# Lightning attention feeding a two-layer network: from the seventh chunk couple on, attention in two TensorE groups per couple, two state buffers, a new order of loads, some early casts on VectorE

## The chip, the cores and the metric

One core of one Trainium2 chip. The metric is the device time of one execution in microseconds (us), as the median of several. Executions of one kernel on one chip mostly agree within a few tenths of a per cent (at the widest the kernel before took 216.96 to 218.66 us on one chip). Chips differ by a few tenths too: the kernel before had medians of 217.1 to 217.9 us in the four sets of runs below. So small differences are read from the ratios to the kernel before on the same chip.

## The reference

Attention with a decaying state over 4 batches, 8 heads, 768 positions of 64 values; its output is 3072 tokens of 512 values, which go through a two-layer network:

```python
intra = einsum(q_block, k_block) * decay_mask        # "s", then the mask
intra = einsum(intra, v_block)                       # "c"
inter = einsum(q_block * lam**(i+1), kv_state)       # "n"
out_block = intra + inter
kv_state = lam**block * kv_state + einsum(k_dec, v)  # "u", then a sum
...
x = out.transpose(...).reshape(3072, 512)
h = x @ w_in                                         # 512 x 2048: first layer, L1
g = where(h >= 1, h, where(h <= -1, 0, (h+1)**2/4))  # relu on ScalarE, rest on VectorE
return g @ w_out                                     # 2048 x 512: second layer, L2
```

## The kernel before

The kernel takes 24 chunks of 128 positions as 12 couples m = 0 to 11, two per stage of the network from couple 0 on (stage 0 is couples 0 and 1, and so on). The program is written by a list scheduler in Python: every piece of work is an operation with an engine, a modelled duration, what it needs and a due time, and the modelled time at which it starts sets its place in its engine's queue. On the chip only the queues and the semaphores count.

Small matmuls of attention run in a 64x64 tiling, in groups. Before, each couple from 1 on had three: A (n of one half and the scores of one chunk), B (the other scores and n), C (scores times v, from couple 3 on with the state product u of the next couple; the first four products are groups of their own). A block, below, is what the first layer puts into one buffer (four matmuls of 512 columns or eight of 256), or four 512-wide matmuls of the second layer.

```python
def f_u(m):                                   # state product of couple m
    ...
        pl, nm = (..., ((pp_s, "ps"), (pp_t, "pt")))[min(m, 2)][i]
        pu[i] = pl.tile([128, HP, D], F32, name=nm, tag=nm)
    ...                                       # 32 (or 16) matmuls of 64x64

def f_sum(c):                                 # VectorE: PSUM -> state
    if c % NCB == 0:
        nc.vector.tensor_copy(state, pu[c % 2])
    else:
        nc.vector.tensor_tensor(state, state, pu[c % 2], op=AX.add)

def f_ub(c):                                  # ScalarE: bf16 copy of the state, read by n
    ...
    nc.scalar.copy(out=ub[c % NUB], in_=state)
...
# what an L1 block needs: its xT, its weights, and the relu two blocks back (two "ph" buffers)
[("x", ...), ("w", 0, ...), ("m", 1, 0) if n1 < 2 else ("r", n1 - 2), ("l1", n1 - 1)]
...
# due times run backwards from the users of a result
d = [u.due - u.ns - x.extra - LAT for u in users[x.key] if not u.dma]
x.due = min(d + ([x.own] if x.own is not None else []), default=1e9)
```

PSUM, the memory into which every matmul of this kernel writes and from which ScalarE and VectorE read, is full with eight buffers: two "ph" (first layer), two "py" (second layer), "ps" and "pt" (scores or state product, one each), two "px" (attention's output, which ScalarE casts to xT, the first layer's input). In the profile, sc are the masked scores, gT is the second layer's input and osb the output copy.

## Time and profile before

217.12 us median of six (217.03 to 217.34). Marks of TensorE's timeline:

| mark | before, us |
|---|---|
| first L2 block starts | 37.27 |
| group A of couple 5 starts | 82.83 |
| end of the span | 215.8 |
| waits of TensorE for another engine after 38 us | 0.3 |

Profile lines have the source line of the kernel that they belong to (L441), the engine, the operation, what it writes and reads, and in brackets what ended the idle time ahead of it. TensorE (PE) is busy to the end, and after 38 us it waits for almost nothing.

### The profile page before, as it was taken

What the parts mean: (1) busy time and instruction counts of PE and PEld (TensorE: products, weight loads), DVE (VectorE), ACT (ScalarE), POOL (GpSimd) and SP (SyncE); (2) the same over time, 40 slices, a digit from 0 to 9 for tenths busy, and PEclk for the clock granted to TensorE, in tenths of its full rate; (3) what the DMA queues carried; (4) which work ended last, traced back from release to release, by engine and by line L of the source; (5) the groups of instructions that cost most, each with busy time, mean ns of one, the idle gap of its engine ahead of it and who ended that gap; (6) DMA issues with size and microseconds to landing.
All of it is one profiled execution on the core that took longest, in us unless ns stands there. A gap on an engine that the chain in (4) does not pass through costs nothing.

```text
span 215.8 us, 5410 instructions
## 1 busy us (share of the span) xinstructions
PE 202.4 (94%) x2285; PEld 117.6 (54%) x2314; DVE 150.3 (70%) x235; ACT 116.5 (54%) x201; POOL 55.6 (26%) x60
## 2 busy tenths in 40 slices
PE   6887897999999999999999999999999999999993
PEld 4455685666646777667544444544544444444442
DVE  4684887998961999689999688775666655464301
ACT  3556686348536677662956547664644544555020
POOL 4070260069252844267154008000000000000000
PEclk9999999999999999999999999999999999999999
DMA  5999999999998999899998956621101101110022
GB/s 158 290 218 201 271 191 196 226 294 242 166 284 176 243 246 217 203 227 283 242 202 226 263 135 209 101 73 52 49 0 52 49 3 49 49 49 21 31 97 97
DMA packets 64586, 34.43 MB, mean 160 GB/s; under 512 B 20402, under 2 KB 61618, under 8 KB 64562
## 3 DMA queue, kind: packets, MB, share of 16 engines
q1 hardware_dynamic: 60336, 29.89, 62.1%
q0 software_dynamic: 4224, 4.19, 12.4%
q8 instruction: 18, 0.29, 0.6%
q14 instruction: 6, 0.05, 0.1%
q10 hardware_dynamic: 2, 0.00, 0.0%
HBM read 27.26 MB, written 6.29 MB: 155 GB/s over the span
## 4 chain that ended last, share of the span: by engine, by line
PE 88%; DVE 6%; issue 2%; ACT 2%; POOL 0%; POOLq 0%; DVEq 0%
PE ph L441 37%; PE py L489 35%; PE ph L151 3%; PE px L390 3%; PE ps L362 2%; PE px L374 2%; DVE sc L423 2%; PE py L483 1%; PE ps L403 1%; DVE w L466 1%; DVE ks L294 1%; ACT xT L430 1%; ACT qT L334 1%; PE pt L324 1%; DVE gT L471 1%
## 5 line engine op out<-in xcount | busy, mean ns | idle before, releaser
L441 PE MATMUL ph<-xT,w_in_sb 128*128 128x256 bf16 (+1 forms) x570 | 94.5, 308 | 1.3 <-ACT xT L430 1.1
L450 ACT ACTIVATE r<-ph,one 128x512 bf16<-128x512 f32 x96 | 65.7, 688 | 52.5 <-PE ph L441 46.8
L489 PE MATMUL py<-w_out_sb,gT 128*128 128x512 bf16 x345 | 86.5, 379 | 2.4 <-issue 1.7
L441 PEld LDWEIGHTS <-w_in_sb 128*128 128x128 bf16 x576 | 54.9, 98 | 31.2 <-issue 1.2
L489 PEld LDWEIGHTS <-gT 128*128 128x128 bf16 x368 | 34.5, 98 | 37.8
L460 DVE TENSOR_SCALAR t<-r 128x1024 bf16<-128x1024 bf16 x48 | 25.8, 538 | 22.0 <-ACT r L450 22.0
L471 DVE TENSOR_TENSOR gT<-w,t 128x1024 bf16<-128x1024 bf16 x48 | 39.9, 832 | 1.3
L466 DVE TENSOR_TENSOR w<-r,t 128x1024 bf16<-128x1024 bf16 x48 | 39.0, 813 | 1.4
L302 POOL TENSOR_TENSOR qs<-x0f,tab_q 128x512 bf16<-128x512 f32 x21 | 24.4, 1181 | 41.5 <-DMA x0f<-in_q_dram 32.4
L294 POOL TENSOR_TENSOR ks<-x1f,tab_p 128x512 bf16<-128x512 f32 x18 | 22.8, 1284 | 25.7 <-PE pt L403 21.1
L423 DVE TENSOR_TENSOR sc<-ps,causal 128x512 bf16<-128x512 f32 x23 | 15.9, 689 | 14.1 <-PE pt L362 12.4
L494 ACT COPY osb<-py 128x512 f32<-128x512 f32 x23 | 13.5, 585 | 17.3 <-PE py L489 15.3
L430 ACT CAST xT<-px 128x512 bf16<-128x512 f32 x24 | 13.1, 586 | 9.5 <-PE px L390 8.6
L423 DVE TENSOR_TENSOR sc<-pt,causal 128x512 bf16<-128x512 f32 x22 | 15.0, 680 | 0.0
L317 ACT CAST v<-x2f 128x512 bf16<-128x512 f32 x24 | 13.7, 619 | 0.2
L151 PE MATMUL ph<-ident 128*128 128x512 bf16 (+1 forms) x39 | 9.5, 381 | 1.6 <-POOL ident masks.py:199 1.6
L362 PE MATMUL ps<-qT,kT 64*64 64x128 bf16 x184 | 10.8, 220 | 0.0
L418 ACT CAST ub<-state 128x256 bf16<-128x256 f32 x19 | 7.7, 406 | 5.0 <-DVE state L411 3.5
L362 PEld LDWEIGHTS <-kT 64*64 64x64 bf16 x384 | 7.8, 106 | 4.0 <-issue 3.8
L362 PE MATMUL pt<-qT,kT 64*64 64x128 bf16 x176 | 9.8, 219 | 0.0
L374 PE MATMUL px<-qT,ub 64*64 64x128 bf16 x152 | 6.4, 222 | 2.0 <-ACT xT L430 1.9
L390 PEld LDWEIGHTS <-v 64*64 64x64 bf16 x384 | 5.8, 106 | 4.5 <-issue 4.4
(59 smaller groups left out, 84.6 us busy)
## 6 DMA issues: line engine op xcount, KB each, us to landing
x0f<-in_q_dram SPq DMA_DIRECT2D x12, 512.0 KB, 6.7
x1f<-in_k_dram SPq DMA_DIRECT2D x12, 512.0 KB, 6.2
x2f<-in_v_dram SPq DMA_DIRECT2D x12, 512.0 KB, 7.0
out_dram<-osb SPq DMA_DIRECT2D x23, 256.0 KB, 2.3
w_in_sb<-in_moe_w_in_dram POOLq DMA_DIRECT2D x4, 512.0 KB, 6.6
w_out_sb<-in_moe_w_out_dram POOLq DMA_DIRECT2D x4, 512.0 KB, 11.0
kT<-ks SPq DMA_TRANSPOSE x18, 4.0
out_dram<-osb SPq DMA_DIRECT2D x1, 192.0 KB, 1.9
```

The source lines that it names most:

```text
L151: nc.tensor.matmul(hot[0][:, :w], lhsT=ident, rhs=_bc(ident, 1, w // 128), start=True, stop=True)
L294: eng.tensor_tensor(ho(ks[c])[:, bs], hs(qkv_ld[c, 1])[:, bs], ho(_bc(tab, 2, D))[:, bs], op=AX.mult)
L302: eng.tensor_tensor(ho(qs[m, e])[:, bs], hs(qkv_ld[m, 0][:, :, e])[:, bs], ho(_bc(tab_q[:, e, m % (NCB // 2), :], 2, D))[:, bs], op=AX.mult)
L362: nc.tensor.matmul(pst[a, r][HD[i], b, :], lhsT=kT[a][HD[r], b, HD[i]], rhs=q_cols(2 * m + i, b, HD[r]), start=True, stop=True)
L423: nc.vector.tensor_tensor(sc_sb[c][:, g], pst[c, g], _bc(causal2[:, c % 2], 1, HP), op=AX.mult)
L430: nc.scalar.copy(out=o, in_=px[:, c % 2].rearrange("p h (e j) -> p h j e", e=2))
L441: nc.tensor.matmul(ph[:, j * m:(j + 1) * m], lhsT=w_in_sb[:, ko, (ni + j) * 128:(ni + j + 1) * 128], rhs=xT[s][:, ko, tok], start=(ko == 0 ...
L450: nc.scalar.activation(out=o, in_=x, func=AF.Relu, bias=one[:, 0:1])
L460: nc.vector.tensor_scalar(t, r, 0.5, 1.0, op0=AX.mult, op1=AX.min)
L466: nc.vector.tensor_tensor(w, r, t, op=AX.subtract)
L471: nc.vector.tensor_tensor(gT[s][:, f - RW * n:f, tok].rearrange("p (a b) m -> p a b m", a=RW), w.rearrange("p a (b m) -> p a b m", m=m), t ...
L489: nc.tensor.matmul(py_t[s, ms], lhsT=gT[s][:, ko, ms * 128:(ms + 1) * 128], rhs=w_out_sb[:, ko, :], start=(ko == 0), stop=(ko == FO - 1))
```

## The change

Its intent, as the diff reads: six tiling-mode groups fewer, since each costs time beside its matmuls; a state sum that need not wait for the copy of the last one; and a start with less on ScalarE (two copies of kT, not shown, move to VectorE as well). Cut to its core:

```diff
+    PAIRED = 6
-    ORDER = [0, 1, (0, 0), ...]                 # order of the loads
+    ORDER = [('lq', 0), ('lk', 0), ...]
+    V_DVE, X_DVE, UB_DVE = (2,3,4,5), (0,1), (2,3)
-    state = const.tile([128, HP, D], F32)
+    state = [const.tile([128, HP, D], F32, name=f"state{i}") for i in range(2)]
-    LDD, STD = 25000, 3000                      # due times of loads, groups, transposes ...
+    LDD, STD = 16000, 3000
...
 def f_u(m):
+            ... ((pp_h, "ph"), (pp_y, "py")))[3 if m >= PAIRED else min(m, 2)][i]
+def f_b(m, more):
+    if m < PAIRED:
+        f_s(2 * m + 1, 1)
+    else:
+        f_n(m, 1); f_s(2 * m + 1)
+    if more: f_u(m + 1)                          # u moves from group C into group B
...
 def f_ub(c):
+    src = pu[0] if c % NCB == 0 else state[c % 2]   # first chunk of a batch: straight from PSUM
...
-    PARTS = {1: 2, 2: 2, 4: 1}
+    PARTS = {1: 2, 2: 2, 3: 2, 4: 1}             # L1 of stage 3 in 256-wide halves
```

From couple 6 on the groups are B (n, scores, u of the next couple) and C (scores times v, n, scores of the next couple). Scores of the next couple now live in "ps" and "pt" while u is made, so u goes to "ph" and "py".

## The prediction

> **What bounds the kernel now.** I read the page first (shares, slices, chain), then the TensorE's waits from 38 us on, then its timeline row by row.
>
> ```profile
> span 215.8 us, 5410 instructions
> ...
> PE 202.4 (94%) x2285; PEld 117.6 (54%) x2314; DVE 150.3 (70%) x235; ACT 116.5 (54%) x201; POOL 55.6 (26%) x60
> ...
> PE   6887897999999999999999999999999999999993
> ...
> PE 88%; DVE 6%; issue 2%; ACT 2%; POOL 0%; POOLq 0%; DVEq 0%
> ```
>
> TensorE is the bound. Only the first eight slices (43 us) have holes; after them it works to the end. What it waited for, first over the whole run, then from 38 us on (us in total, times, longest):
>
> ```profile
> PE px L374 <- ACT xT L430: 1.9, 2, 1.5
> ...
> PE ph L441 <- ACT xT L430: 1.1, 1, 1.1
> PE pt L324 <- ACT qT L334: 0.7, 1, 0.7
> PE pt L331 <- ACT qT L334: 0.7, 1, 0.7
> ```
> ```profile
> PE py L489 <- issue: 1.7, 11, 0.2
> PE px L374 <- ACT xT L430: 0.3, 1, 0.3
> ```
>
> So after 38 us a wait of TensorE for another engine costs 0.3 us in all. What an attention group costs is read from the starts of the rows around it:
>
> ```profile
> 161.37 1.03 PE L441 MATMUL ph<-xT,w_in_sb 128*128 128x512 bf16 x4
> 162.32 0.31 PE L374 MATMUL px<-qT,ub 64*64 64x128 bf16 x8
> ...
> 166.34 0.24 PE L362 MATMUL ps<-qT,kT 64*64 64x128 bf16 x1
> ...
> 166.81 1.04 PE L489 MATMUL py<-w_out_sb,gT 128*128 128x512 bf16 x4
> ...
> 169.50 0.64 PE L390 MATMUL px<-sc,v 64*64 64x128 bf16 x32
> 170.07 1.04 PE L441 MATMUL ph<-xT,w_in_sb 128*128 128x512 bf16 x4
> ```
>
> Four 512-wide matmuls take 0.86 us where one feed-forward block follows another, but 0.95 (161.37 to 162.32) where a 64x64 group follows. The group of 32 value products takes 0.57 us (169.50 to 170.07); eight steps of four parallel tiles at 0.053 us (128 columns, a quarter of 0.216) would be 0.43. The group of 16 score and 8 state products takes 0.47 (166.34 to 166.81) for six steps, 0.32. So each group costs 0.09 on entering and 0.14 inside, some 0.235 us, for being a group.
>
> Last, how fast ScalarE frees a PSUM buffer:
>
> ```profile
> 139.31 1.07 ACT L430 CAST xT<-px 128x512 bf16<-128x512 f32 x2
> 140.27 1.15 ACT L317 CAST v<-x2f 128x512 bf16<-128x512 f32 x2
> ...
> 142.88 0.40 ACT L418 CAST ub<-state 128x256 bf16<-128x256 f32 x1
> ...
> 144.90 0.69 ACT L450 ACTIVATE r<-ph,one 128x512 bf16<-128x512 f32 x1 [0.73 <-PE ph L441]
> ```
>
> The first-layer block behind the last row began at 143.77: its relu starts 1.1 us after the block's start and ends 0.69 later. TensorE follows 0.05 after a release (xT ended at 26.07, the matmul started at 26.12). A buffer is therefore reusable 1.83 us after its block began; a block lasts 0.86. With two "ph" buffers that is hidden; with one it is not.
>
> **What the Trainium skill says.** "TensorEngine Tiling (Array Packing)", Key Properties: changing the tiling mode drains TensorE. The trace agrees, with the 0.235 us above. "PSUM — Partial Sum Buffer", Terms and Engine vs sequencer instructions: eight banks, a matmul's output stays within one, ScalarE's and VectorE's queues are strict FIFO and matmuls complete in program order. The kernel uses all eight (ph 2, py 2, pt, ps, px 2), so a new tile in "ph" takes a buffer from the first layer. The trace before shows the FIFO order (the casts above stand ahead of relus), but never a lack of "ph".
>
> **The change, part by part.**
>
> 1. Groups. Couples 6 to 11 had three each (n+s, s+n, c with the next u; s scores, n query times state, c scores times v, u the state product). Now two: s+n with the next u; c with the next s and n. Matmuls are the same. Six groups fewer: 6 x 0.235 = -1.4 us, all on the path.
>
> 2. Early order. The first L1 block now comes before the score group of couple 1; its xT casts move to VectorE, where they queue behind two k casts, two v casts and a q cast. Adding VectorE's rows (masks 0.61 each, casts 0.65, copies 0.4) I get the second xT at 18.7 us and L1 at 18.8 instead of 19.18; but the group of 0.46 us that was done then now follows, so nothing is won. The 1.1 us wait for xT stays (the next L1 really needs it now). The two qT waits (0.67 each) go, since L1 blocks now stand between the transposes. About -1.4 us by the first second-layer block.
>
> 3. First layer of stage 3 in 256-wide halves: 16 matmuls take 1.75 us where 8 wide ones take 1.73; eight times, +0.15. The small waits at 100-104 us (0.45 with issue) should go: -0.45.
>
> 4. The cost. For couples 6 to 11 the state product is put in "ph" and "py" instead of "ps" and "pt", as these now hold scores. In the built program I looked up which bank each tile has and what each wait names. While the product of couple 6 is held, three L1 blocks in a row get the same bank. Hand arithmetic with the durations above:
> - Couple 6: the first L1 after the group waits for a relu that stands behind the ub copy, which waits for the group: 0.1+0.31+0.69+0.05 = 1.15. Two L1 in one bank with four L2 matmuls between: 1.83-1.72 = 0.11. Two directly: 1.83-0.86 = 0.97. Then an L2 block takes the "py" buffer that an output copy must first empty, and this copy stands behind two xT and two v casts that follow group c: release 3.45 after c starts, against 1.65 of own work: 1.8.
> - Couple 7: 0.3 (a relu behind a ub copy), 0.97, 0.11, then L1 waits for a relu behind an output copy and two xT casts: 2.6-0.84 = 1.76.
> - Couple 8: 0.11 + 0.45. Couple 9: about 0.2 (masks on VectorE ahead of the state copy). Couple 10: an L1 waits for a relu behind an output copy: 3.2-1.72 = 1.48. Couple 11: 0.11.
> Sum: 4.0 + 3.1 + 0.6 + 0.2 + 1.5 + 0.1 = 9.5 us. TensorE has no slack there, so all of it is on the path.
>
> 5. Two state buffers let the second sum start without waiting for the first's ub copy: shorter holding, no path. The v and state casts on VectorE early on only shift load; the DMA has its loads and transposes landed 1 to 2 us before the new, earlier use (for couple 6: 87.1 in the trace before, used at about 89).
>
> Sum: 217.05 - 1.4 - 1.4 + 0.15 - 0.45 + 9.5 = 223.4; I say 223.2.
>
> **Rivals.** (a) The plan works: no buffer waits, only parts 1 to 3: 217.05 - 3.1 = 214.0. For it: the change is plainly meant so, and its many constants look tuned. Against: the waits are in the program, engines are in order, and the scheduler's need list for L1 and L2 blocks doesn't name the state product as a holder of their buffer. (b) The start is the main effect, for instance VectorE, busy 15.1 of the 19 us from 19 to 38, becomes the bound there by the moved casts: some 1.5 us of casts could cost 1 to 2 and take the qT gain away: 225. Against: its idle time there (1.3 us before 27.8) covers most. (c) Only the direct single-buffer waits bite, while ScalarE, 54% busy, has its casts done sooner than I think: stalls of 5 us, total 219. For it: a stall early shifts what follows and may hide the next. Against: the long ones hang on casts that cannot start before group c ends.
>
> **Range and chances.** The sum of the gains is sure to about 1 us, that of the stalls to about 2.5. That gives 219.6 to 226.5. Slower by over 2% begins at 221.4, a little under the middle: 0.70. Within 2% needs rival (c) or (a): 0.27. Faster by over 2% (under 212.7) would need more than all gains and no stall: 0.03.
>
> **What would show it.** In the changed kernel's waits from 80 us on: TensorE's L1 line waiting for ScalarE's relu by 6 to 7 us in about a dozen waits, and its L2 line for the output copy, one of about 1.8 us. The 64x64 groups from couple 6 on: two per couple, 0.7 and 0.9 us long. TensorE's slices 16 to 30 no longer all 9. Before 80 us: no wait of transposes for qT, the first L2 block at about 35.9 (37.27 before). It is wrong if the L1 waits are under 3 us, or if the start moves by more than 2 us either way.

## The result, and the profile after

223.34 us median of six (223.13 to 224.61) against 217.12: a ratio of 1.0295, 95% interval 1.0271 to 1.0319. (A ratio is the mean time of one kernel's runs over that of the other's in the same rounds, so not quite the ratio of the medians quoted. Executions over 1.5% slower than the fastest of the same kernel are left out of the means.) All runs were at a granted clock of 0.997 or above.

The page of the changed kernel, its shares and TensorE's 40 slices of 5.5 us:

```profile
PE 203.7 (92%) x2356; PEld 124.4 (56%) x2382; DVE 152.0 (69%) x245; ACT 110.8 (50%) x191; POOL 53.5 (24%) x60
...
PE   7889799999999997778799999799999999999994
```

Slices 16 to 20 (83 to 110 us) and 26 (138 to 144) have holes that were not there. What TensorE waited for from 38 us on (total, times, longest):

```profile
PE ph L457 <- ACT r L466: 5.9, 6, 1.5
PE py L505 <- ACT osb L510: 1.5, 1, 1.5
PE py L505 <- issue: 0.6, 4, 0.2
```

L457 is the first layer, L466 its relu, L505 the second layer, L510 the output copy: 7.4 us of waits for ScalarE that free a PSUM buffer, where there had been none. The first of these waits, in TensorE's timeline after group B of couple 5 (which ends with u of couple 6):

```profile
85.61 1.03 PE L457 MATMUL ph<-xT,w_in_sb 128*128 128x256 bf16 x8 [1.14 <-ACT r L466]
86.70 0.81 PE L505 MATMUL py<-w_out_sb,gT 128*128 128x512 bf16 x3
87.42 1.03 PE L457 MATMUL ph<-xT,w_in_sb 128*128 128x256 bf16 x8
89.28 1.03 PE L457 MATMUL ph<-xT,w_in_sb 128*128 128x256 bf16 x8 [0.82 <-ACT r L466]
...
95.31 1.02 PE L505 MATMUL py<-w_out_sb,gT 128*128 128x512 bf16 x4 [1.50 <-ACT osb L510]
```

The first-layer blocks at 87.42 and 89.28 have no other block between them: their starts are 1.86 apart, where 0.86 would be the block alone. They share one buffer, since the other is held. By whom, VectorE's timeline shows:

```profile
92.88 0.69 DVE L439 TENSOR_TENSOR sc<-ps,causal 128x512 bf16<-128x512 f32 x1 [0.67 <-PE pt L364]
93.49 0.41 DVE L424 COPY state<-ph 128x256 f32<-128x256 f32 x1
93.82 0.68 DVE L439 TENSOR_TENSOR sc<-pt,causal 128x512 bf16<-128x512 f32 x1
94.42 0.41 DVE L426 TENSOR_TENSOR state<-state,py 128x256 f32<-128x256 f32 x1
```

The state copy that empties "ph" stands between two masks (L439). They mask the scores of couple 6, which are made in group C of couple 5; that group began at 91.97. The product had been done at about 84.5. VectorE's own queue thus holds a first-layer buffer for 9 us, though the copy takes 0.41. It was put there by the scheduler: the sum is needed only by the next n, two groups later, so its due time is late, and nothing tells the scheduler that a buffer of the first layer hangs on it.

By the marks:

| mark | before | after | difference |
|---|---|---|---|
| first L2 block | 37.27 | 35.69 | -1.58 |
| A of couple 5 | 82.83 | 81.35 | -1.48 |
| from there to the end | 132.97 | 140.05 | +7.08 |

The marks add up to 5.6 us, the medians differ by 6.2: the profiled execution of the kernel before took 217.55 us, 0.4 above its median, that of the changed kernel 223.13. So the marks of the start may be some tenths too good for the changed kernel.

### The profile page after: what moved, and what is told of

Its sections match the earlier page's. It is cut to its first block, busy times and chain, and to the rows that moved or that the text cites. A ratio compares the mean times of both kernels' runs of the same rounds, so it can differ in the third digit from the quotient of the medians.

```text
span 221.4 us, 5549 instructions
## 1 busy us (share of the span) xinstructions
PE 203.7 (92%) x2356; PEld 124.4 (56%) x2382; DVE 152.0 (69%) x245; ACT 110.8 (50%) x191; POOL 53.5 (24%) x60
## 4 chain that ended last, share of the span: by engine, by line
PE 50%; issue 2%; ACT 2%; DVE 0%
PE py L505 24%; PE ph L457 21%; PE px L395 1%; ACT r L466 1%; PE py L499 1%; PE ps L364 1%; PE px L377 1%; PE ph L499 0%; PE ph L409 0%; ACT xT L446 0%; PE pt L364 0%; PE py L409 0%; DVE osb L517 0%; ACT osb L510 0%
## 5 line engine op out<-in xcount | busy, mean ns | idle before, releaser
L457 PE MATMUL ph<-xT,w_in_sb 128*128 128x256 bf16 (+1 forms) x635 | 95.4, 293 | 7.4 <-ACT r L466 5.9
L466 ACT ACTIVATE r<-ph,one 128x512 bf16<-128x512 f32 x96 | 65.8, 688 | 59.0 <-PE ph L457 42.8
L505 PE MATMUL py<-w_out_sb,gT 128*128 128x512 bf16 x347 | 86.7, 379 | 3.1 <-ACT osb L510 1.5
L457 PEld LDWEIGHTS <-w_in_sb 128*128 128x128 bf16 x640 | 61.1, 98 | 34.0 <-issue 8.7
L505 PEld LDWEIGHTS <-gT 128*128 128x128 bf16 x368 | 35.3, 98 | 38.4 <-issue 1.8
L482 DVE TENSOR_TENSOR w<-r,t 128x1024 bf16<-128x1024 bf16 x48 | 40.9, 853 | 1.5
L487 DVE TENSOR_TENSOR gT<-w,t 128x1024 bf16<-128x1024 bf16 x48 | 38.5, 801 | 1.5
L476 DVE TENSOR_SCALAR t<-r 128x1024 bf16<-128x1024 bf16 x48 | 24.3, 507 | 20.7 <-ACT r L466 20.5
L439 DVE TENSOR_TENSOR sc<-ps,causal 128x512 bf16<-128x512 f32 x23 | 15.9, 690 | 24.9 <-PE pt L364 19.1
L296 POOL TENSOR_TENSOR ks<-x1f,tab_p 128x512 bf16<-128x512 f32 x18 | 21.0, 1189 | 15.9 <-PE ph L409 8.3
L510 ACT COPY osb<-py 128x512 f32<-128x512 f32 x23 | 13.5, 586 | 18.3 <-PE py L505 17.3
L446 ACT CAST xT<-px 128x512 bf16<-128x512 f32 x22 | 11.9, 588 | 8.4 <-PE px L395 7.0
L439 DVE TENSOR_TENSOR sc<-pt,causal 128x512 bf16<-128x512 f32 x22 | 15.0, 682 | 0.0
L319 ACT CAST v<-x2f 128x512 bf16<-128x512 f32 x20 | 11.6, 621 | 1.4 <-PE px L395 0.9
L364 PE MATMUL ps<-qT,kT 64*64 64x128 bf16 x184 | 9.7, 218 | 0.0
L395 PE MATMUL px<-sc,v 64*64 64x128 bf16 x384 | 8.6, 219 | 0.6 <-DVE sc L439 0.6
L434 ACT CAST ub<-state 128x256 bf16<-128x256 f32 x14 | 5.6, 402 | 5.1 <-DVE state L426 5.1
```

The lines of the kernel that those rows point to most:

```text
L296: eng.tensor_tensor(ho(ks[c])[:, bs], hs(qkv_ld[c, 1])[:, bs], ho(_bc(tab, 2, D))[:, bs], op=AX.mult)
L364: nc.tensor.matmul(pst[a, r][HD[i], b, :], lhsT=kT[a][HD[r], b, HD[i]], rhs=q_cols(2 * m + i, b, HD[r]), start=True, stop=True)
L395: nc.tensor.matmul(px[HD[g], i, j, :], lhsT=v_sb[(2 * m + e) % NV][HD[i], 2 * j + g, :], rhs=sc_sb[2 * m + e][HD[i], r, b, :], start=(c % ...
L439: nc.vector.tensor_tensor(sc_sb[c][:, g], pst[c, g], _bc(causal2[:, c % 2], 1, HP), op=AX.mult)
L457: nc.tensor.matmul(ph[:, j * m:(j + 1) * m], lhsT=w_in_sb[:, ko, (ni + j) * 128:(ni + j + 1) * 128], rhs=xT[s][:, ko, tok], start=(ko == 0 ...
L466: nc.scalar.activation(out=o, in_=x, func=AF.Relu, bias=one[:, 0:1])
```

## The experiments

The theory was that the held buffers cost about 8.9 us after couple 5 (8.3 in single stalls that the trace shows, the rest in many of 0.1), that six groups fewer give 1.4 back and the start gives 1.5. Rivals: the longer groups themselves, or a changeover into pairing, cost the time; VectorE has no room; the start is the cost. All twelve runs gave correct results. Edits are against the changed kernel.

### Pairing off, pairing alone, pairing later, stage 3 as before

```diff
# e1_three_groups
-    PAIRED = 6
+    PAIRED = 12
# e2_pair_only: all constants of the start and PARTS as before the change, and
-    V_DVE, X_DVE, UB_DVE = (2,3,4,5), (0,1), (2,3)
+    V_DVE, X_DVE, UB_DVE = (), (), ()
# e3_pair_from_8
-    PAIRED = 6
+    PAIRED = 8
# e4_stage3_wide
-    PARTS = {1: 2, 2: 2, 3: 2, 4: 1}
+    PARTS = {1: 2, 2: 2, 4: 1}
```

> The changed kernel with three groups for every couple; its new order of loads, early casts, two state buffers and 256-wide stage 3 stay. Theory (the state product held in the first and second layers' PSUM buffers costs some 8.9 us, six groups fewer give back 1.4, the start gives 1.5): 223.3 - 8.9 + 1.4 = 215.8, within 1.2, with the waits of the first and second layer for ScalarE after 38 us under 1 us together. Rival (the start, with casts on VectorE, or the two state buffers slow it): stays above 221.

Measured: 216.54 us (ratio to before 0.9958, interval 0.9942 to 0.9975). Waits of L1 and L2 for ScalarE after 38 us: 0.3. The start, with the halves of stage 3, is no cost but a gain, of 0.9 by the ratio; pairing is the cost, 6.8 us by the medians and 7.3 by the ratios. The run is 0.7 above the expectation: the gain of the start is smaller than the 1.5 of the theory, and the stalls are too (the table below).

> The changed kernel with all constants of the start put back (order of loads, due times, v, x and state casts on ScalarE, stage 3 in whole blocks): pairing and two state buffers are left. Theory: 217.1 + 8.9 - 1.4 = 224.6, within 2, since other due times move which blocks meet a held buffer; first-layer waits for relu of 5 us or more after 80 us. Rival (the start is the cost): 217 or less.

Measured: 223.05 us (1.027; 1.024 to 1.030). The start undone, the loss stays, 1.5 below the middle of the expectation and within its range. The second sign, waits of 5 us or more for relu, did not come. The waits have other names here: of the first layer's 5.8 us after 38 us, 3.2 are for the state copies themselves, 1.6 for relu, 1.0 for xT.

> The changed kernel with pairing from couple 8 on in place of 6. Theory: the stalls of couples 6 and 7 (3.9 and 2.9 us by the trace) go and two groups (0.47) come back: 223.3 - 6.8 + 0.5 = 217.0, within 1.5. Rival 1 (each pairing costs the same, by its longer groups: 7.1 us over six couples, 1.2 each): 223.3 - 2.4 = 220.9. Rival 2 (the first paired couple pays for the changeover, wherever it lies): about 220.

Measured: 215.93 us (0.9928; 0.9912 to 0.9944), 1.1 below the middle of the expectation, within its range, and below three groups. Neither rival fits: four couples are still paired, and a changeover is still there. In the trace only 0.3 us of first-layer waits for ScalarE are left after 38 us. So even the stall of 1.4 us that the changed kernel had at couple 10 is gone, although couple 10 is still paired.

Yet the copies come late here too. Two rows of TensorE's timeline and one of VectorE's:

```profile
115.09 1.05 PE L457 MATMUL ph<-xT,w_in_sb 128*128 128x256 bf16 x8
116.92 1.03 PE L457 MATMUL ph<-xT,w_in_sb 128*128 128x256 bf16 x8
121.00 0.41 DVE L426 TENSOR_TENSOR state<-state,ph 128x256 f32<-128x256 f32 x1
```

The product of couple 8 was done at about 115.2, so its buffer was held for 6 us, and no block waited for it: a second-layer block stands between the two first-layer blocks, and their starts, 1.83 apart, are about as far as one buffer needs. A held buffer thus cost time here only where the order of blocks asked for the other one sooner.

> The changed kernel with the first layer of stage 3 in whole 512-wide blocks again. Theory (halving costs 0.15 us of matmul time and the stalls hang on the buffers, not on the width): 223.2, within 0.8. Rival (the halved blocks with their later inputs meet the held buffers and make the stalls of couples 6 and 7): 219 or less.

Measured: 223.04 us (1.0251; 1.0183 to 1.0319), but in two pairs, 221.4 to 221.8 and 224.3 to 224.4 (the trace is one of the slower pair). All four are above the 219 of the rival, so the width is not the cause; what sets the pairs apart was not found. Which wait shows the cost does change, as TensorE's waits from 38 us on tell (two more, not shown, are 1.0 for xT and 0.6 for issue):

```profile
PE ph L457 <- DVE state L426: 4.4, 3, 2.8
PE ph L457 <- DVE state L424: 3.2, 2, 2.2
```

With other blocks in between, a first-layer block is given the state product's own buffer and waits for the state copy itself (7.6 us in all), instead of for the relu in the one other buffer. The holder is the same, only the name differs.

### The state copies first

If holding is what costs, it must be enough to move the copies in VectorE's queue, with groups, matmuls and buffers as they are. One line in the scheduler, after all due times are set, does it (cut to the lines that matter; e6 also changes the need of ub accordingly):

```diff
# e5_copies_first: state sums from couple 6 on get due = -1
-        left = {x.key: len(x.needs) for x in ops}
+        left = {x.key: (len(x.needs), setattr(x, 'due', -1 if x.key[0] == 'sum'
+                and x.key[1] >= 2 * PAIRED else x.due))[0] for x in ops}
# e6_copies_first_ub: that, and ub of a batch's first chunk reads the state copy
-        src = pu[0] if c % NCB == 0 else state[c % 2]
+        src = pu[0] if c % NCB == 0 and c // 2 < PAIRED else state[c % 2]
# e7_from_8: e6 with PAIRED = 8;   e8_from_4: e6 with PAIRED = 4
```

> The changed kernel, with the copy of the state product (the state sums of couples 6 to 11) put at the head of what VectorE may do next, so that it stands ahead of the masks and not behind the masks of the following group; groups, matmuls and PSUM buffers are those of the changed kernel. Theory (it is the holding time of the state product in the first and second layers' buffers that costs): in the built program the first-layer blocks now alternate between their two buffers but for one (after group B of couple 5 a block gets the state product's own buffer, held to the end of the state copy and of a ub copy, about 1 us): 223.3 - 8.9 + 1.0 = 215.4, within 1.2; first-layer waits for relu under 1 us. Rival A (the longer groups themselves cost): 221 or more. Rival B (copies ahead of masks make the value products wait for the masks): 218 to 221, with waits of px for sc of 2 us or more.

Measured: 216.46 us (0.9952; 0.9926 to 0.9978), within the theory's range, 1.1 above its middle. Moving copies of 0.4 us in a queue takes 6.9 us off the changed kernel by the medians (7.4 by the ratios): all that was lost, and a little more. VectorE and TensorE at the place shown above:

```profile
84.92 0.42 DVE L424 COPY state<-ph 128x256 f32<-128x256 f32 x1 [1.18 <-ACT ub L434]
85.44 0.42 DVE L426 TENSOR_TENSOR state<-state,py 128x256 f32<-128x256 f32 x1
85.78 0.68 DVE L487 TENSOR_TENSOR gT<-w,t 128x1024 bf16<-128x1024 bf16 x1
86.39 0.68 DVE L439 TENSOR_TENSOR sc<-ps,causal 128x512 bf16<-128x512 f32 x1
```
```profile
85.39 1.03 PE L457 MATMUL ph<-xT,w_in_sb 128*128 128x256 bf16 x8 [1.02 <-DVE state L424]
86.48 0.81 PE L505 MATMUL py<-w_out_sb,gT 128*128 128x512 bf16 x3
87.13 1.91 PE L457 MATMUL ph<-xT,w_in_sb 128*128 128x256 bf16 x16
88.87 1.03 PE L505 MATMUL py<-w_out_sb,gT 128*128 128x512 bf16 x4
```

The copy now starts at 84.92 instead of 93.49, and the two blocks that were 1.86 apart run as one row of 16 matmuls from 87.13 on. They still stand side by side, so here it is the release that does it. Some blocks did move, since the modelled times of VectorE's work enter into the whole schedule: group C of couple 5 now follows one second-layer block, not two. What that is worth was not tested by itself. The masks come 0.8 us later than before (86.39 against 85.57) and nobody waits for them: waits of px for sc are 0.6 us over the whole run, as in the changed kernel. Rivals A and B fall, as far as a cost of this size goes. The first block, after the group, still waits 1.02 us for the copy.

> The run before, and the ub copy of a batch's first chunk reads the state copy and not the PSUM buffer, so that ScalarE no longer holds that buffer. Theory: the one remaining stall after group B of couple 5 falls from about 1 us to about 0.5: 0.3 to 0.7 us less than the run before, 214.9. Rivals as there.

Measured: 216.22 us (0.9947; 0.9924 to 0.9970), 0.24 below the run before where 0.3 to 0.7 was expected (a difference inside the noise), and 1.3 above the figure given. The wait fell from 1.02 to 0.66 us in the traces, as it should. A second of 0.4 (group B of couple 10, then a block that waits for relu) and the 0.3 for xT stay. So six pairs, with their stalls, are no better than three groups by anything that these runs resolve (ratios 0.9947 and 0.9958, with overlapping intervals).

> The same with pairing from couple 8 on. Theory: two groups more (2 x 0.235 = 0.47) and without the stall of about 0.5 after group B of couple 5: the same within 0.3 as the run with pairing from 6, and 0.2 to 0.4 less than pairing from 8 without the two mends (215.9). Rival (pairing gains nothing by itself, groups cost no 0.235): equal to three groups everywhere, 216.5.

Measured: 215.96 us (0.9929; 0.9902 to 0.9957): within 0.3 of pairing from 6, as expected, and no better than pairing from 8 without the mends (0.9928), where I expected 0.2 to 0.4. There was no stall left to mend. The rival, equal to three groups everywhere, is not quite excluded (0.9929 and 0.9958, with intervals that just overlap).

> The same with pairing from couple 4 on. Theory: two groups fewer than from 6 (-0.47), and in the built program the block after every group B gets the free buffer, so the stall of 0.5 goes: 214.9 - 0.47 - 0.4 = 214.0, within 0.8. Rival (in stage 2 VectorE and the loads have no room, so copies or masks come late): 215 or more.

Measured: 216.96 us as the median of five runs (0.9976 of before; 216.93 to 217.25), 3 us above the expectation: a clear miss. The first execution, the profiled one, took 1173.84 us and says nothing on this; it is told at the end.

### The start in two halves, pairing from 7, and pairing from 4

```diff
# e9_casts_back: PAIRED = 12, and
-    V_DVE, X_DVE, UB_DVE = (2,3,4,5), (0,1), (2,3)
+    V_DVE, X_DVE, UB_DVE = (), (), ()
# e10_order_back: PAIRED = 12, casts stay; ORDER, D0, LDD, QXD, AD, BD, UD, TD, W_AFTER as before the change
# e11_from_7: e6 with PAIRED = 7
# e12_from_4_look: e8 unchanged
```

> Three groups for every couple with the new order of loads and due times, but the early v, x and state casts back on ScalarE. The prediction held that these casts only shift load: then as the run with three groups, 216.5, within 0.6. Rival (the casts on VectorE are what brings the first-layer blocks forward): the start's gain of 1.1 to 1.4 us goes, 217.6 or more, first second-layer block after 36.5 us.

Measured: 216.91 us, ratio 0.9959 (0.9938 to 0.9979), on a chip on which the kernel before took 217.87; three groups with the casts on VectorE had 0.9958. The casts by themselves are worth nothing measurable. The second half of the rival's sign did appear (first L2 block at 38.27 us) without its cost: 128 first-layer matmuls are done ahead of it instead of 112. The first L2 block is thus a poor mark where the order of blocks changes.

> Three groups for every couple with the casts on VectorE, but the order of loads and the due times of before. Theory (the gain of the start is from the order, which sets first-layer blocks between the transposes; in this program one such block still stands between the two query transposes): most of the gain goes, 217.0 to 217.8, first second-layer block at 36.5 us or later. Rival (it is the casts): 216.5 or less.

Measured: 217.95 us, ratio 1.0016 (0.9986 to 1.0046), just above the expected 217.0 to 217.8, with the first second-layer block at 36.93 us. Against 0.9958 that is 0.0058 of 217.3, or 1.3 us, with an interval of about 0.5 to 2.0 (two of its four executions took 218.4 and 218.6, at a granted clock of 0.992, the others 217.3 and 217.5): the gain of the start lies in the order of loads and due times, as far as these runs tell. A wait of 1.9 us of the first L1 block for its xT and one of 0.7 for qT are in this trace and not in that of three groups with the new order.

> Copies first and ub from the state copy, pairing from couple 7 on. In the built program the block after every group B gets the free first-layer buffer. Theory: one pair more than from 8 (-0.22 by the trace) and no stall after group B: 215.7, within 0.4. Rival (a stall of 0.5 or more appears at the changeover wherever it lies): 216.3 or more.

Measured: 215.67 us, ratio 0.9904 (0.9885 to 0.9924): as expected, and the best kernel. It beats the changed kernel by 3.4% by the medians (3.8% by the ratios) and the kernel before by 1%. All that TensorE waited for from 38 us on:

```profile
PE ph L457 <- ACT xT L446: 0.3, 1, 0.3
PE ph L457 <- ACT r L466: 0.2, 1, 0.2
```

> The kernel of the run with pairing from couple 4 again, whose profiled execution was a disturbed one (1172 us) while five others took 217.0. Expected: 217.0, with 512-wide matmuls at 0.216 us; the 3 us above the expectation of 214.0 must show between 60 and 85 us as waits for copies, casts or loads if the theory of VectorE's room in stage 2 is right, or as waits of first-layer blocks for relu if it is the buffers again.

Measured: 217.68 us (two runs; ratio 0.9993, 0.9962 to 1.0024), matmuls at their usual 0.216 us. TensorE's waits from 38 us on, and one row of its timeline:

```profile
PE ph L457 <- ACT xT L446: 2.2, 3, 1.0
PE ph L457 <- DVE state L424: 0.8, 1, 0.8
```
```profile
80.80 1.47 PE L457 MATMUL ph<-xT,w_in_sb 128*128 128x256 bf16 x12 [0.95 <-ACT xT L446]
```

Neither of the two guesses was right in the main. Two waits of 0.95 us are for xT: in couples 3 and 4 a first-layer block that needs the couple's own attention output follows group C directly, and the cast to xT needs C's value products. By the trace it is the placing of C, too close to its user, and not VectorE's room; no run tested this. The third wait, 0.8, is the held buffer again. Together they are 2.7 us, most of the miss of 3.

## Why the prediction was right, point by point

The mechanism was right, and so was the size of the whole: 223.2 predicted, 223.3 measured. That the figures agree to 0.1 is luck, though: the gains were put at 3.1 and came to about 2.0 (0.9 for all but the groups by e1, 1.1 for the groups), the stalls were put at 9.5 and came to about 8.2. The terms of its sum one by one (a couple's stalls are those while its state product is held):

| term | predicted | found |
|---|---|---|
| six groups fewer | -1.4 | about -1.1, an estimate: B and C of a couple take 1.62 to 1.65 us in the trace (0.71 or 0.74, by the size of u, + 0.91), A, B and C in that of e1 1.74 (0.46 + 0.46 + 0.82); with 0.09 to enter each, about 0.2 per couple |
| start | -1.4 | -1.5 at couple 5's group A in the profiled executions, -0.9 in the times of e1 (with the next two terms); 1.3 from the order by e10, 0 from the casts by e9 |
| halves in stage 3 | +0.15 | not resolved: e4 spreads over 3 us |
| small waits at 100 to 104 us | -0.45 | none of them in the trace after |
| couple 6: 1.15, 0.97, 1.8 | +4.0 with 0.11 | 1.18, 0.99, 1.66 (start to start, over the normal step) |
| couple 7: 0.3, 0.97, 1.76 | +3.1 with 0.11 | at most 0.2, 0.99, 1.60 |
| couple 8: 0.45 | +0.6 with 0.11 | 0.42 |
| couple 10 | +1.5 | 1.42 |
| all stalls | +9.5 | 8.3 in single ones, 7.9 to 8.4 by e1 (6.8 to 7.3 of pairing and 1.1 of groups) |

The single-buffer interval was met: 1.86 between the starts at 87.42 and 89.28. (The 1.83 is slightly mis-added. Its own rows give 1.13 + 0.69 + 0.05 = 1.87.) "TensorE has no slack there, so all of it is on the path" is borne out by e5, which shortens the holding, with few other moves, and gets the time back. Of its signs, the first second-layer block (35.69, 35.9 said) and the groups came as said. The waits for relu were 5.9 us, but in six waits and not in a dozen, and of the waits of transposes for qT 0.2 us stayed, besides the 0.5 at the very start that it had not listed.

Three things the prediction did not see. First, it took the held buffer from the built program, and saw from the need list that the scheduler does not know of it, but did not ask what kept it held. The reason, a copy of 0.41 us behind the masks of the next group, is what a mend must change, and e5 did so with one line; for couple 9 alone the prediction spoke of masks ahead of a state copy. Second, it listed the stalls couple by couple. They hang on the order of blocks: pairing from 8 lost the stall at couple 10 as well. Third, rival (a), that the plan works as meant, it gave at 214.0. With the holding mended the plan came to 215.7 to 216.2. Against three groups with the same start (0.9958) pairing from 7 is worth 1.2 us by the ratios (0.9 by the medians); pairing from 6 is worth nothing that these runs resolve, since the 1.1 that six groups save stands against stalls of 0.7 and 0.4 that remain.

Of its rivals, (a) falls with the result, (b), VectorE's early load as the bound, with e1 and e9. (c), that only the direct single-buffer waits bite, falls with the trace: waits behind xT casts and output copies were 1.60, 1.66 and 1.42 us.

One test was not possible. To put the state product in "ph" and "py" without pairing, so as to see the buffers alone, makes a program that is refused as a deadlock when it is built, so there is no run of it; my reading, not tested, is that a first-layer block then waits for a state copy that stands on VectorE behind masks of a group that comes after that block. The effect of the buffers without the groups is therefore known only from the other side, by e5.

## What to carry to other kernels

When a tile is moved into a buffer that a busy pipeline rotates through, ask when it is let go, not how long its use lasts. Here copies of 0.41 us, placed late in VectorE's queue, held a buffer for up to 9 us each and together cost the kernel about 7 us. Ask also what is to run meanwhile: the same kind of buffer held for 6 us in e3 cost nothing, because no two first-layer blocks stood side by side there. The Trainium skill's "Perfetto Trace Analysis", Matmuls, asks for independent matmul groups to rotate through different PSUM banks so that emptying one overlaps the next; the trace agrees (0.86 us a block with two buffers, 1.86 with one), and a borrower takes part in that rotation. A scheduler that works from due times needs to know of it, either as a need of the blocks or as an early due time of the copy. And judge merged groups by what they move closer together too: in the trace, pairing from couple 4 lost 1.9 us to casts that had no time left.

## What the Trainium skill lacked or had wrong

- "TensorE: Matmul & The Clock Gate", Part 1, has the array at full or half clock, with a peak-current limit at 13/16 and a note of a clock stuck at a quarter for 50 us and more. One execution here (the first of pairing from 4) ran its matmuls at about a sixth of the usual rate from its first ones at 1.6 us to its end: about 1.3 us for each 512-wide matmul where 0.216 is normal, 1172 us in all, with VectorE, ScalarE and GpSimd at about their usual busy times. Why is not known. The granted clock in the records stayed at 1.000, so that column does not show it; the step between matmuls does. Five other executions on the same chip were normal. Its shares, and two rows of its timeline:

```profile
PE 1142.7 (97%) x2357; PEld 425.6 (36%) x2382; DVE 143.2 (12%) x245; ACT 113.5 (10%) x191; POOL 50.6 (4%) x60
```
```profile
158.47 4.35 PE L505 MATMUL py<-w_out_sb,gT 128*128 128x512 bf16 x3
162.49 8.19 PE L457 MATMUL ph<-xT,w_in_sb 128*128 128x256 bf16 x12
```

- "TensorEngine Tiling (Array Packing)", Key Properties, says that a change of tiling mode drains TensorE, and has no figure for it. Here a group costs about 0.09 us on entering and, by the pairs, about 0.2 us in all.
- "PSUM — Partial Sum Buffer" has the banks and the order of the queues, but no figure for how soon a bank can be used again. Here it was 1.86 us from the start of a block of eight 256-wide matmuls that ScalarE empties by a relu of 0.69 us, so that two banks are needed where blocks of 0.86 follow each other directly.
